# Narrower column tiles for three groups of small matmuls, with a reordered task list, in a polynomial-sketch attention and mixture-of-experts attention kernel

## The chip, the core and the metric

The kernel runs on one core of a Trainium2 chip. A core has five engines that run side by side and wait for each other through semaphores: TensorE (PE, matmuls), VectorE (DVE), ScalarE (ACT), GpSimd (POOL) and SyncE (SP, which here only issues transfers). The metric is the device time of one launch in microseconds (us). The time before is the median of three runs.

## What is computed

Two stages, for 4 batches of 1088 tokens. The first is a linear attention over 4 heads with sketched features; the second takes its output x (1088 x 128 per batch) through 4 attention experts, of which each token uses 2.

```python
# stage 1: a, b are 8-wide sketches of a token, phi their outer product (64 features)
q_p, k_p = phi(q), phi(k)
kv  = einsum('bhsf,bhsd->bhfd', k_p, v)          # sums over keys
z   = sum(k_p, axis=2)
num = einsum('bhsf,bhfd->bhsd', q_p, kv)         # numerators
den = einsum('bhsf,bhf->bhs', q_p, z) + 1e-6
x   = num / den                                  # heads side by side: (B, S, 128)
# stage 2: for each expert e of the two that a token has chosen
scores = scale * (x wq[e]) (x wk[e])^T           # causal
a      = softmax(scores)
out   += weight_of_e * (a @ (x wv[e]) @ wo[e])
```

## The kernel before

All of it is written for one core, and every engine's instructions are issued in the order of one hand-held list, ORDER. A word of the list is batch.task with arguments: `0.kv` is the task kv of batch 0. There is no scheduler behind it: an engine executes what the list gives it in that order, and waits where something it needs is late. The list mixes the batches, so that the first stage of the next batch lies between the second-stage tasks of this one.

Tasks of the first stage: `bk` and `bq` turn k and q on DVE (lines 338 to 344), `ks` and `qs` make the sketches and features (lines 370 to 411), `kv` sums over keys (kvs, line 424), `tf` turns query features on PE (line 299), `nu` makes numerators and x (numer, line 440, then DVE lines 444 to 447), `tx` turns x. `ga`, `ge` and `gw` choose two experts per token, mostly small operations on DVE and POOL; `mp` and `md` spread the choice as masks; `ld`, `sw` and `sp` issue transfers on SP: load the next batch, save x to memory, and read it back four times as xrep. `eo` and `em` multiply weights once; `warm` is a matmul whose result is not used.

Tasks of the second stage: `cu` (line 556) multiplies x by the experts' matrices and picks the two chosen ones, `s` (lines 595 and 617) makes scores, their maximum (DVE line 570) and exponentials (ACT line 574), `t` turns the weights on DVE (line 278), `vb` and `va` sum the weights times x (values, line 651), `zb` and `o` (line 733) make the output.

PE works in fp32, and each fp32 matmul is two records in the profile, each a load of weights (PEld) and a matmul. A matmul addresses a tile of the 128 x 128 array by the rows of its operands and the columns of its output. The profile writes that shape as rows*columns: `32*128` is a tile of 32 rows and 128 columns. Four tiles of 32*128 can be at work beside each other.

The task kv uses tiles of 128*64: two heads at a time, each with 64 features as weights' columns, over 33 columns of values (32 and a one for the denominator). It is 36 matmuls, 72 records, per batch. The task nu uses tiles of 64*64, 72 matmuls, 144 records, per batch.

The tasks vb and va sum over keys. Keys are split into 34 blocks of 32 tokens, c, and each block into row groups: row group r (rows 32r to 32r+31) holds 32 of every 128 queries, so that the causal end differs by r. Group B holds query tiles 1 to 5 and group A holds tiles 0, 6, 7 and 8, each tile once for each of its two chosen experts (one unit is 32 query columns). For each r and c one matmul takes xrep's block c as weights (32 rows, 128 columns) and moves 32 columns per unit that still needs block c. Towards the last blocks fewer units are left: in group A's last part the matmuls move 160, then 96, then 32 columns; in group B's last part 192, 128, then 64. The order of r is chosen greedily, by the row group that has been given the least time so far; the time counted is the larger of the columns moved and 128. The four parts of a group are the tasks vb:0 to vb:3 and va:0 to va:3, 68 records in vb:3 and 102 in va:3.

Of the kernel before, what the change touches and what calls it, by code (L numbers as in the profile page):

```python
# [19 lines left out]


ORDER = """
    0.bk 0.bq1 0.bq0 0.ks:0:4 0.vk 0.ks:4:9 0.qs:4:9 0.qs:0:4 0.tf:13:18 0.kv 0.eo 1.ld 0.tf:8:13 1.bk 0.tf:0:8
    1.ks:4:9 1.ks:0:4 0.nu:0:4 0.warm:2 0.nu:4:9 0.sw 0.tx:0:4 0.warm:2 1.bq 2.ld 0.warm:2 0.warm:2 0.ga:0:4 0.tx:4:9
    0.ge:0 0.gw:0 1.kv 0.ga:4:9 1.qs:4:9 0.em 0.mp:2:4 0.mp:4:6 1.tf:8:13 1.tf:13:18 0.mp:0:2 0.ge:4 0.sp 0.mp:6:8
    2.bk 0.mp:8:9 1.qs:0:4 2.bq 3.ld 1.nu:5:9 0.cu:4 0.cu:6 0.cu:0 0.gw:4 1.tf:0:8 2.ks:4:9 0.cu:2 0.s:5:1 1.nu:0:5
    2.ks:0:4 0.s:3 0.md 0.s:4:2 0.t:3 1.tx:0:4 0.t:5 0.t:1 2.kv 0.shb 1.tx:4:9 2.qs:4:9 2.qs:0:4 0.cu:8 0.s:7 0.s:8
    0.t:2 2.tf:13:18 0.t:4 1.ga:0:9 1.md 0.t:7 0.s:6:0 0.t:8 0.t:0 0.vb:0 0.vb:1 0.vb:2 0.vb:3 1.ge:0 2.tf:8:13 0.zb:3
    1.sw 1.cu:0 0.t:6 1.cu:4 0.o:3 1.cu:2 1.cu:6 1.s:4:2 0.zb:5 1.s:5:1 1.s:3 0.va:0 0.sha 3.bk 0.va:1 0.va:2 1.t:4
    1.t:5 2.tf:0:8 1.t:2 3.ks:0:4 3.bq 0.va:3 1.sp 1.t:1 2.nu:0:5 0.o:5 0.zb:6 1.cu:8 1.s:7 0.o:6 0.zb:0 2.tx:0:4  # L30
    1.t:3 3.ks:4:9 2.nu:5:9 1.s:6:0 0.zb:1 0.o:0 2.tx:4:9 1.s:8 1.gw:0 1.shb 0.zb:8 3.kv 2.ga:0:9 2.ge:0 1.vb:0 2.md
    2.sw 0.o:8 1.t:7 1.vb:1 3.qs:4:9 1.t:8 3.qs:0:4 1.t:0 1.t:6 1.vb:2 1.vb:3 2.cu:4 2.cu:2 0.o:1 1.zb:5 2.cu:0
    2.s:4:2 2.s:5:1 3.tf:13:18 1.sha 1.zb:3 1.va:0 1.va:1 3.tf:8:13 2.t:4 2.cu:6 1.o:3 1.o:5 2.t:1 3.tf:0:8 2.gw:0
    1.va:2 1.zb:1 2.t:5 1.va:3 3.nu:5:9 2.sp 2.s:3 2.t:2 2.s:6:0 3.nu:0:5 1.o:1 2.shb 2.t:3 3.sw 3.tx:4:9 1.zb:8
    3.tx:0:4 2.s:7 2.t:0 2.cu:8 1.o:8 3.ga:0:9 1.zb:6 1.zb:0 3.md 2.t:7 2.vb:0 2.vb:1 2.s:8 2.vb:2 2.vb:3 1.o:0 3.ge:0
    2.t:6 2.t:8 3.cu:8 3.cu:2 3.cu:4 1.o:6 2.sha 3.cu:0 3.cu:6 3.s:4:2 2.zb:5 3.s:5:1 3.t:2 3.t:1 3.s:3 2.zb:1 3.t:4
    3.t:3 2.o:5 2.zb:3 2.va:0 2.va:1 3.t:5 2.va:2 2.va:3 3.sp 3.s:8 2.o:3 2.o:1 3.gw:0 3.shb 3.t:8 2.zb:0 2.zb:6 3.s:7
    3.s:6:0 3.t:6 2.o:6 2.o:0 3.t:7 3.vb:0 3.vb:1 3.vb:2 3.t:0 3.vb:3 3.zb:1 3.va:0 3.va:1 3.va:2 3.zb:3 3.o:3 3.o:1
    3.shp 3.zb:5 2.zb:8 3.va:3 3.o:5 3.zb:0 2.o:8 3.o:0 3.zb:6 0.warm:2 3.zb:8 3.o:6 3.o:8
"""  # L40


# [1 line left out]
def kernel(  # L44
# [43 lines left out]
    P = ps.tile([128, 8, 512], F32, tag="P", name="P")  # L88
# [239 lines left out]
    def batch(b):  # L328
        if b not in made:
            made[b] = Batch(b)  # L330
        return made[b]
# [82 lines left out]
            in1=a_[:, 0, :, :, None].to_broadcast([128, n, R, R]),  # L414
            op=ALU.mult)

    def kvs(b):
        kp, k0 = batch(b).fp["k"], bank()
        kv = P[:, k0, 0 : 2 * (D + 1)].rearrange("p (m d) -> p m d", m=2)
        for m in range(2):  # L420
            for j in range(NJ):
                for x in range(2):
                    h = 2 * m + x
                    nc.tensor.matmul(kv[64 * x : 64 * x + 64, m], kp[:, j, h], vp[:, j, h, :],  # L424
                                     start=(j == 0), stop=(j == NJ - 1))
        nc.scalar.copy(kvz, kv)

    def turn_features(b, y0, y1, copy=None):
        m_ = batch(b)
# [1 line left out]
                     for y in range(y0, y1)], m_.qpT[:, y0:y1], copy)  # L431

    def numer(b, x0, x1):
        k0, m, qpT = bank(2), 2 * (x1 - x0), batch(b).qpT
        for y in range(2 * x0, 2 * x1):
            c = (D + 1) * (y - 2 * x0)
            for x in range(2):
                for half in (0, 64):
                    rows = slice(64 * x, 64 * x + 64)
                    nc.tensor.matmul(P[half : half + 64, k0 + x, c : c + D + 1], qpT[rows, y, half : half + 64],  # L440
                                     kvz[rows, y % 2], start=True, stop=True)
        den = p2.tile([128, 2, 2 * NJ], F32, tag="den", name=f"den{b}_{x0}")[:, :, 0:m]
        nus = P[:, k0 : k0 + 2, 0 : m * (D + 1)].rearrange("p x (m d) -> p x m d", d=D + 1)
        nc.vector.tensor_scalar_add(den, nus[:, :, :, D], 1e-6)
        nc.vector.reciprocal(den, den)
        for x in range(2):
            nc.vector.tensor_tensor(
                out=xs[:, x0:x1].rearrange("p j (m x d) -> p x (j m) d", m=2, x=2)[:, x], in0=nus[:, x, :, 0:D],
                in1=den[:, x, :, None].to_broadcast([128, m, D]), op=ALU.mult)
# [179 lines left out]
    def values(b, grp, part):  # L629

        tiles, units = GROUPS[grp], UNITS[grp]
        if part == 0:
            k0 = bank(2)
            held.update((k0, k0 + 1))
            k1 = bank(2)
            held.update((k1, k1 + 1))
            sums[grp] = k0, k0 + 1, k1, k1 + 1
        last = {(i, r): min(4 * i + (3 - r if i in BACK else r), NC - 1) for i in tiles for r in range(4)}
        todo = {r: collections.deque(c for c in range(*PARTS[grp][part : part + 2]) if c <= max(last[i, r] for i in tiles))
                for r in range(4)}  # L640
        time = [0] * 4
        while any(todo.values()):

            r = min((r for r in range(4) if todo[r]), key=lambda r: time[r])
            c = todo[r].popleft()
            (c0, _, u0), t = next((p, t) for p, t in zip(parts(grp), aT[grp]) if p[0] <= c < p[1])
            us = [x for x, (i, s) in enumerate(units) if c <= last[i, r]]
            assert us == list(range(us[0], len(units)))
            time[r] += max(32 * len(us), 128)
            rows = slice(32 * r, 32 * r + 32)  # L650
            nc.tensor.matmul(P[:, sums[grp][r], 32 * us[0] : 32 * len(units)], xrep[rows, c], t[rows, c - c0, us[0] - u0 :],  # L651
                             start=(c == 0), stop=(c == max(last[i, r] for i in tiles)), skip_group_check=True)
# [168 lines left out]
```

## Time and profile before

| | |
|---|---|
| median of 3 runs | 286.21 us (285.89 to 287.32) |
| the profiled execution | 287.48 us, its span 285.7 us |
| PE busy | 95% of the span, 4521 records |
| DVE / ACT / POOL busy | 77% / 37% / 21% |
| share of the chain that ended last | PE 78%, DVE 11%, transfers 4% |
| matmuls of values (line 651) | 1800 records |
| matmuls of numer (line 440) / kvs (line 424) | 576 / 288 records |

Times of the profile are microseconds from the start of the span, unless marked ns. A group of instructions is given as line, engine, operation, output<-inputs, tile, shape and type, count, then busy time, mean ns of one, and idle time before them. The chain that ended last follows the work back from the last instruction: each of its pieces has a start, the time by which it moved the end of the chain, and its engine and line. A matmul's record is longer than the time for which it keeps others out, since matmuls are pipelined; the distance between ends is what it costs.

### The profile page before, as it was taken

The page shows a single profiled execution, that of the slowest core. Times are in us where ns is not written, and L with a number is a line of the kernel's source. Part 1 is how long each engine was busy: PE and PEld are TensorE (multiplying, and loading weights), DVE is VectorE, ACT ScalarE, POOL GpSimd, SP SyncE. Part 2 cuts the span into 40 slices and gives each one's busy share as a digit, 9 for nine tenths or more (in the row PEclk, how much of TensorE's full clock was granted, in tenths as well). Part 3 has the DMA queues.
Part 4 walks back from the last instruction along what each step waited for, and adds up shares of the span by engine and source line. Part 5 has one row for each costly group of instructions (what it writes and reads, how often), then busy time and mean ns, then how long its engine had stood idle before and what let it go on. Part 6 is the DMA issues. An engine that isn't in the chain of part 4 may idle for free.

```text
span 285.7 us, 10500 instructions
## 1 busy us (share of the span) xinstructions
PE 272.0 (95%) x4521; PEld 218.3 (76%) x4521; DVE 220.4 (77%) x499; ACT 105.2 (37%) x262; POOL 59.3 (21%) x143
## 2 busy tenths in 40 slices
PE   7789699999999999999999999999999999999993
PEld 2776588756599769877797699678796797589983
DVE  5916859888788988988594968885988997986541
ACT  2242373384533282055212542353133622250110
POOL 8516052323311002221460021003001001000100
PEclk9979959999999999999999999999999999999999
DMA  6930999803415002692157032994433108923011
GB/s 211 266 71 22 286 184 193 187 7 126 96 31 177 21 0 71 125 181 48 33 94 196 8 49 50 164 165 97 105 122 66 22 11 156 181 52 91 12 39 38
DMA packets 41086, 28.94 MB, mean 101 GB/s; under 512 B 7504, under 2 KB 39504, under 8 KB 41040
## 3 DMA queue, kind: packets, MB, share of 16 engines
q1 hardware_dynamic: 41024, 28.28, 45.9%
q8 instruction: 35, 0.57, 0.9%
q14 instruction: 11, 0.09, 0.1%
q10 hardware_dynamic: 16, 0.00, 0.0%
HBM read 23.66 MB, written 4.60 MB: 99 GB/s over the span
## 4 chain that ended last, share of the span: by engine, by line
PE 78%; DVE 11%; DMA 4%; issue 2%; POOL 2%; ACT 0%; SPq 0%; POOLq 0%; DVEq 0%; ACTq 0%
PE P L651 23%; PE P L595 22%; PE P L733 10%; PE P L556 9%; PE P L440 3%; PE P L299 3%; PE P L401 2%; PE P L617 2%; DMA mk<-dm 2%; PE P L424 2%; DVE qT L344 2%; DMA dm<-sel 1%; DVE zT L726 1%; DVE a L570 1%; POOL qp L411 1%
## 5 line engine op out<-in xcount | busy, mean ns | idle before, releaser
L574 ACT ACTIVATE a<-a,mx 128x768 f32<-128x768 f32 (+8 forms) x68 | 53.8, 791 | 67.0 <-DVE mx L570 56.7
L595 PE MATMUL P<-xT,uT 128*128 128x512 f32 (+3 forms) x192 | 64.9, 490 | 0.2
L595 PEld LDWEIGHTS P<-xT,uT 128*128 128x128 f32 x192 | 34.0, 190 | 26.4 <-issue 18.4
L651 PE MATMUL P<-aTA,xrep 32*128 32x160 f32 (+3 forms) x1080 | 39.1, 295 | 0.0
L651 PEld LDWEIGHTS P<-aTA,xrep 32*128 32x128 f32 x1080 | 37.9, 185 | 1.3 <-DVE mx L570 0.8
L733 PEld LDWEIGHTS P<-mo,zT 128*128 128x128 f32 (+1 forms) x288 | 33.9, 185 | 4.6 <-issue 1.9
L733 PE MATMUL P<-mo,zT 128*128 128x128 f32 (+1 forms) x288 | 36.6, 279 | 0.8 <-DVE zT L726 0.7
L651 PE MATMUL P<-aTB,xrep 32*128 32x320 f32 (+4 forms) x720 | 37.2, 348 | 0.0
L570 DVE CUSTOM_DVE_ANT_0 a<-P,mask 128x768 f32<-128x768 f32 (+3 forms) x32 | 32.4, 1018 | 4.4 <-PE P L595 4.0
L651 PEld LDWEIGHTS P<-aTB,xrep 32*128 32x128 f32 x720 | 33.1, 185 | 3.3 <-issue 1.0
L556 PE MATMUL P<-xT,mcat 128*128 128x256 f32 (+1 forms) x160 | 33.6, 361 | 0.0
L556 PEld LDWEIGHTS P<-xT,mcat 128*128 128x128 f32 x160 | 27.5, 190 | 3.7 <-issue 0.5
L278 DVE STREAM_TRANSPOSE aTA<-a 128x256 f32<-128x256 f32 (+4 forms) x28 | 24.4, 916 | 1.6 <-ACT a L574 1.6
L278 DVE STREAM_TRANSPOSE aTB<-a 128x1024 f32<-128x1024 f32 (+3 forms) x28 | 24.4, 910 | 0.5 <-ACT a L574 0.5
L562 DVE COPY_PREDICATED uT<-mk,P 128x512 f32<-128x512 uint8 (+1 forms) x30 | 18.5, 637 | 7.7 <-DMA mk<-dm 4.6
L736 ACT COPY ob<-P 128x256 f32<-128x256 f32 (+2 forms) x24 | 7.5, 313 | 39.6 <-PE P L733 36.3
L726 DVE COPY_PREDICATED zT<-mk,yT 128x768 f32<-128x768 uint8 (+2 forms) x24 | 18.6, 775 | 3.9 <-POOL zT L723 1.7
L724 DVE TENSOR_TENSOR zT<-yT,mk 128x768 f32<-128x768 f32 (+2 forms) x24 | 17.0, 710 | 3.0 <-PE P L733 2.9
L411 POOL TENSOR_TENSOR kp<-kab 128x1280 f32<-128x1280 f32 (+1 forms) x6 | 13.0, 2173 | 21.1 <-DVE kab L408 12.9
L558 ACT COPY uT<-P 128x512 f32<-128x512 f32 (+1 forms) x20 | 10.3, 522 | 16.3 <-PE P L556 16.2
L570 DVE CUSTOM_DVE_ANT_0 a<-P,mask_back 128x256 f32<-128x256 f32 (+3 forms) x32 | 15.2, 484 | 0.0
L411 POOL TENSOR_TENSOR qp<-qab 128x1280 f32<-128x1280 f32 (+1 forms) x6 | 12.9, 2173 | 8.5 <-DVE qab L408 5.9
(190 smaller groups left out, 298.8 us busy)
## 6 DMA issues: line engine op xcount, KB each, us to landing
xrep<-dx SPq DMA_DIRECT2D x16, 544.0 KB, 9.0
mk<-dm SPq DMA_DIRECT2D x4, 864.0 KB, 6.0
kin<-in_k_dram SPq DMA_DIRECT2D x4, 544.0 KB, 4.1
qin<-in_q_dram SPq DMA_DIRECT2D x4, 544.0 KB, 8.0
vin<-in_v_dram SPq DMA_DIRECT2D x16, 128.0 KB, 6.8
dx<-xs SPq DMA_DIRECT2D x4, 512.0 KB, 6.6
out_dram<-ob SPq DMA_DIRECT2D x64, 16.0 KB, 2.1
out_dram<-ob SPq DMA_DIRECT2D x16, 64.0 KB, 1.6
```

The lines of the kernel that those rows point to most:

```text
L278: nc.vector.transpose(t[:, 0 : c1 - c0, n - u0 : n - u0 + s].rearrange("p c s k -> p s c k"), a[:, :, 32 * c0 : 32 * c1].rearrange("p s (c ...
L411: eng.tensor_tensor(out=fp[:, j0:j1].rearrange("p j h (x y) -> p (j h) x y", y=R), in0=a_[:, 1, :, None, :].to_broadcast([128, n, R, R]), ...
L556: nc.tensor.matmul(P[:, k0 + x // 2, x % 2 * w : x % 2 * w + w], mcat[:, e], queries, start=True, stop=True)
L558: nc.scalar.copy(u.rearrange("p t s q -> p s t q"), P[:, k0, 0 : 2 * w].rearrange("p (s t q) -> p s t q", s=2, t=n))
L562: nc.vector.copy_predicated(u, mk[:, :, :, x].bitcast(U8), c[:, :, None].to_broadcast([128, n, 2, q]))
L570: nc.vector.tensor_tensor_reduce(out=dst, in0=src, in1=msk, scale=-1.0, scalar=most, op0=ALU.add, op1=ALU.min, accum_out=mx)
L574: nc.scalar.activation(out=a, in_=a, func=ACTF.Exp, bias=mx, scale=-1.0, accum_out=z)
L595: nc.tensor.matmul(flat[:, f + c : f + c + n], turned(b, i)[:, s], m_.xT[:, c - at[i] : c - at[i] + n], start=True, stop=True)
L651: nc.tensor.matmul(P[:, sums[grp][r], 32 * us[0] : 32 * len(units)], xrep[rows, c], t[rows, c - c0, us[0] - u0 :], start=(c == 0), stop=(c ...
L724: nc.vector.tensor_tensor(out=z[:, :, 0:X], in0=y[:, :, 0, None].to_broadcast([128, n, X, nq]), in1=mk[:, :, 0:X], op=ALU.mult)
L726: nc.vector.copy_predicated(z[:, :, 1:], mk[:, :, X:].bitcast(U8), y[:, :, 1, None].to_broadcast([128, n, X, nq]))
L733: nc.tensor.matmul(P[0:nq, k0, DM * t : DM * t + DM], self.zT[:, t, e], mo[:, e], start=(e == 0), stop=(e == E - 1))
```

## The change

Three tasks use narrower tiles, and the list is new.

kvs and numer take 32 columns of weights at a time for batches 1 to 3 (batch 0 keeps 64): kv is 72 matmuls of 128*32 instead of 36 of 128*64, and nu 144 of 64*32 instead of 72 of 64*64 per batch. The task kv may be given in two halves (`1.kv:0:1`, `1.kv:1:2`), each with its own copy to kvz.

In values, where one unit is left, the 128 columns of xrep are taken as four matmuls of 32*32; where two or three are left, as two of 32*64; else as before. The time counted in choosing the row group is now the columns moved, without the floor of 128. Its matmuls per batch go from 34 to 50 in vb:3 and from 51 to 106 in va:3; the other parts are unchanged.

The list has the same tasks in another order, with three `warm` words instead of five and kv of the later batches in halves. Batch 0's `vk` and `kv` are earlier, `eo`, the second half of its gate (`0.ga:0:4`) and part of its masks later, after the first `cu`; the loads of batches 2 and 3 are issued on SP ahead of batch 0's `sw` and `sp`. Behind batch 3's last `va:3` stand 3.zb:0, 2.o:6, 3.o:0, 3.zb:6, 3.o:6, 3.zb:8 and 3.o:8, where there were also 3.o:5, 2.o:8 and a `warm`.

```diff
 ORDER = """
-    0.bk 0.bq1 0.bq0 0.ks:0:4 0.vk 0.ks:4:9 0.qs:4:9 0.qs:0:4 0.tf:13:18 0.kv 0.eo 1.ld 0.tf:8:13 1.bk 0.tf:0:8
-    1.ks:4:9 1.ks:0:4 0.nu:0:4 0.warm:2 0.nu:4:9 0.sw 0.tx:0:4 0.warm:2 1.bq 2.ld 0.warm:2 0.warm:2 0.ga:0:4 0.tx:4:9
-    0.ge:0 0.gw:0 1.kv 0.ga:4:9 1.qs:4:9 0.em 0.mp:2:4 0.mp:4:6 1.tf:8:13 1.tf:13:18 0.mp:0:2 0.ge:4 0.sp 0.mp:6:8
-    2.bk 0.mp:8:9 1.qs:0:4 2.bq 3.ld 1.nu:5:9 0.cu:4 0.cu:6 0.cu:0 0.gw:4 1.tf:0:8 2.ks:4:9 0.cu:2 0.s:5:1 1.nu:0:5
+    0.bk 0.vk 0.bq0 0.warm:2 0.warm:2 0.bq1 0.ks:0:4 0.ks:4:9 0.qs:4:9 0.qs:0:4 0.kv 1.ld 0.tf:8:13 0.tf:13:18
+    0.tf:0:8 0.nu:4:9 0.em 1.bk 1.ks:0:4 1.ks:4:9 1.bq 0.tx:4:9 2.ld 0.nu:0:4 0.ga:4:9 0.ge:4 1.kv:0:1 0.tx:0:4
+    0.mp:4:6 0.mp:6:8 0.gw:4 1.kv:1:2 2.bk 1.qs:0:4 1.qs:4:9 2.bq 3.ld 0.cu:6 0.cu:4 0.ga:0:4 0.eo 1.tf:13:18 1.tf:0:8
+    0.mp:8:9 0.sw 0.mp:0:2 0.sp 1.tf:8:13 0.ge:0 0.mp:2:4 0.gw:0 0.cu:2 2.ks:0:4 0.cu:0 2.ks:4:9 1.nu:5:9 1.nu:0:5
...
-    def kvs(b):
-        kp, k0 = batch(b).fp["k"], bank()
+    def kvs(b, m0=0, m1=2):
+
+        kp, k0, w = batch(b).fp["k"], bank(), 32 if b else 64
...
-        for m in range(2):
+        for m in range(m0, m1):
             for j in range(NJ):
-                for x in range(2):
-                    h = 2 * m + x
-                    nc.tensor.matmul(kv[64 * x : 64 * x + 64, m], kp[:, j, h], vp[:, j, h, :],
+                for x in range(0, 128, w):
+                    h = 2 * m + x // 64
+                    nc.tensor.matmul(kv[x : x + w, m], kp[:, j, h, x % 64 : x % 64 + w], vp[:, j, h, :],
                                      start=(j == 0), stop=(j == NJ - 1))
-        nc.scalar.copy(kvz, kv)
+        nc.scalar.copy(kvz[:, m0:m1], kv[:, m0:m1])
...
-            for x in range(2):
-                for half in (0, 64):
+            for q in range(0, 128, w):
+                for x in range(2):
                     rows = slice(64 * x, 64 * x + 64)
-                    nc.tensor.matmul(P[half : half + 64, k0 + x, c : c + D + 1], qpT[rows, y, half : half + 64],
+                    nc.tensor.matmul(P[q : q + w, k0 + x, c : c + D + 1], qpT[rows, y, q : q + w],
                                      kvz[rows, y % 2], start=True, stop=True)
...
-            time[r] += max(32 * len(us), 128)
-            rows = slice(32 * r, 32 * r + 32)
-            nc.tensor.matmul(P[:, sums[grp][r], 32 * us[0] : 32 * len(units)], xrep[rows, c], t[rows, c - c0, us[0] - u0 :],
-                             start=(c == 0), stop=(c == max(last[i, r] for i in tiles)), skip_group_check=True)
+            time[r] += 32 * len(us)
+            rows, w = slice(32 * r, 32 * r + 32), {1: 32, 2: 64, 3: 64}.get(len(us), 128)
+            for d in range(0, DM, w):
+                nc.tensor.matmul(P[d : d + w, sums[grp][r], 32 * us[0] : 32 * len(units)], xrep[rows, c, d : d + w],
+                                 t[rows, c - c0, us[0] - u0 :], start=(c == 0), stop=(c == max(last[i, r] for i in tiles)),
+                                 skip_group_check=True)
```

## The prediction

> **What bounds the kernel now.** I read the page's busy shares and slices first, then busy times by stretch, then the chain that ended last, then groups by shape, then single records where one tile shape follows another.
>
> ```profile
> PE 272.0 (95%) x4521; PEld 218.3 (76%) x4521; DVE 220.4 (77%) x499; ACT 105.2 (37%) x262; POOL 59.3 (21%) x143
> PE   7789699999999999999999999999999999999993
> PEclk9979959999999999999999999999999999999999
> ```
>
> TensorE has holes only in the first six slices and at the end. The stretches show it (columns: stretch, its length, busy time of PE, PEld, DVE, ACT, POOL, clock, transfers):
>
> ```profile
> 43.40:78.20 34.80, 34.80 (x512) 23.85 (x512) 30.59 (x77) 18.55 (x46) 11.82 (x11) 1.00 0.56 122
> 180.00:230.00 50.00, 50.00 (x609) 38.43 (x605) 41.72 (x95) 21.25 (x53) 4.78 (x20) 1.00 0.51 104
> 230.00:278.00 48.00, 47.96 (x799) 41.34 (x795) 35.34 (x63) 10.15 (x27) 3.50 (x18) 1.00 0.43 81
> ```
>
> From 43.4 to 278 us PE never stops, at full clock, and no other engine does. So a PE microsecond added there is a microsecond of the span, and its savings count too as long as DVE (42 of 50 us at most) keeps up.
>
> Now what a matmul costs. The chain's pieces (start, time by which the end moved, what):
>
> ```profile
> 56.80 0.49 PE P L401 x32
> 112.17 0.62 PE P L401 x32
> 117.46 1.09 PE P L733 x8
> 226.02 0.89 PE P L733 x8
> 63.05 2.22 PE P L424 x72
> 73.96 0.71 PE P L476 x63
> 125.80 0.91 PE P L440 x64
> 226.91 9.34 PE P L651 x249
> ```
>
> The reader should compare equal work after different neighbours. The 32 records of L401 (64*64) take 0.49 us behind numer (also 64*64), 0.62 behind L299 (64*128). The 8 records of L733 (128*128) take 0.89 behind scores of the same shape, 1.09 behind numer. A change of shape costs 0.13 us into 64 columns and 0.20 into 128, also where only the columns differ (64*128 to 64*64). The records show why:
>
> ```profile
> 73.54 0.41 PE L299 MATMUL P<-ident,qp 64*128 64x64 f32 x8
> 73.89 0.21 PE L476 MATMUL P<-wg,xT 128*32 128x4 f32 x3
> 73.61 0.20 PEld L299 LDWEIGHTS P<-ident,qp 64*128 64x128 f32 x4
> 73.88 0.12 PEld L476 LDWEIGHTS P<-wg,xT 128*32 128x32 f32 x3
> ```
>
> The new shape's first weights load at 73.88, after all matmuls of the old one have started and 0.07 us before the last ends. In every change of shape after 43 us, also between the 128-column and 64-column outputs of L733, it is this 0.07 us. Within one shape, loads run ahead of matmuls. The first 32-column result comes at about 74.08, 0.12 us after the old shape's end (73.96).
>
> ```profile
> L651 PE MATMUL P<-aTA,xrep 32*128 32x96 f32 x128 | 7.3, 266 | 0.0
> L651 PE MATMUL P<-aTA,xrep 32*128 32x32 f32 x104 | 5.4, 263 | 0.0
> ```
>
> Matmuls of 32 columns take as long as those of 96 (263 and 266 ns): the 128 weight columns set the pace. That waste is what the change is about.
>
> **Part 1, the narrow ends of values.** First the pace. Batch 2's group A (four parts, 9.34 us less one entry of 0.2) moves in its busiest row group 1184+1120+1120+1888 = 5312 columns, each matmul counted as at least 128: 1.7 ns a column. In va:3 it has by the loop 7 matmuls of 160, 4 of 96 and 2 of 32 columns: 7x160 + 4x128 + 2x128 = 1888, times 1.7 = 3.2 us, and va:3 indeed lasts 3.0 to 3.4. Without the floor it is 7x160 + 4x96 + 2x32 = 1568, or 2.7. For vb:3 1280 becomes 1024: 2.2 to 1.7. Were that all, the four batches would save 4 x (0.55 + 0.45) = 3.9 us.
>
> But the greedy choice interleaves row groups that are at different widths. I worked va:3's loop through: 16 matmuls of 128 columns, then single ones or pairs whose widths run 64, 128, 64, 128, 64, 128, 64, 32, 64, 32, 64, 32, 64, 32, 64, 32, 64, 32, 64, 32, 64, 32. These are 22 changes of shape per part: 3 into 128, 11 into 64, 8 into 32. vb:3 has 5: 2 into 128, 3 into 64.
>
> If each change waits as in the records above, va:3 becomes a row of short stretches. Entries: 3x0.20 + 11x0.14 + 8x0.12 = 3.1 us (0.14 between 0.13 and the 0.16 that numer's 64 records pay elsewhere). Work inside, that of the busiest row group: 128 columns 4x0.267 + 3x0.267 = 1.87; 64 columns at 96 moved, two records of 0.08 each, 10 stretches with one matmul and one with two, 1.92; 32 columns, at 33 ns a record (L476: (0.71-0.12) over 72 records on four tiles) and 7 ns from one tile to the next, four stretches of one, three of two, one of three matmuls: 4x0.087 + 3x0.153 + 0.22 = 1.03. With 0.1 for the second halves: 8.0 us, against 3.2. Plus 4.8 per batch, 19.2 in all.
>
> vb:3: entries 2x0.20 + 3x0.14 = 0.82; 128 columns 0.96 + 2x0.21; 64 columns at 61 ns a record (0.49 us over 8 rounds of four), busiest row groups 1, 2 and 4 matmuls, 14 records, 0.85: 3.05, against 2.1. Plus 0.95 per batch, 3.8 in all. Part 1: **+23.0 us**. Nothing hides it, PE being full. Ends: -3.9 (a change among column widths costs nothing), and with the entries a quarter dearer, 4 x 3.9 x 0.25 = 3.9 more, +27.
>
> [...] The trace has no 32-row tile beside one of another width; for 64 and 128 rows it shows the drain.
>
> **Part 2, kvs.** Now 72 records at 2.22 us with entry. New: 144 records of 128*32, four tiles; the nearest row is L476 (128*32, 4 columns moved instead of 33): 0.59/72 = 8.2 ns a record, so 1.18 + 0.12 = 1.3. Saves 0.9, three times, 2.7; the halves are apart for batches 1 and 3, two entries more: **-2.4**. Ends: at 61/4 ns as for 64 columns 144 records take 2.2 and save nothing; at L476's pace without entries -3.
>
> **Part 3, numer.** Now 64 records in 0.91 and 80 in 1.30 us, 144 records. New: 288 records on eight tiles; a start follows another by about 7 ns at best in this trace (8.2 for L476), so 2.0 to 2.4 plus two entries, against 2.2: **0**, ends -0.5 and +1.5 for the three batches. The matmul stream is then limited by starts, so halving the width saves nothing.
> [...]
>
> **Part 4, the list.** Changes of shape between tasks go from 82 to 84: +0.3. At the start, the page's groups show PE idle for 8.7 us, before L543 (2.1, behind the gate's selb on DVE), L370 (1.7), L160 (1.1), L299 (0.9 and 0.6), L424, L466 and L440. The first two starts stay. The new list lets `cu` begin after one half of the gate, but puts eo, 0.ga:0:4, two tf's, masks and 1.nu:5:9 behind it, about 8 us of PE work, and on DVE kT (1.45) and qT (2.25) of batch 1 now stand between numer and the gate. Following the DVE order by hand, I get the first `cu` near 33 us instead of 43.4 and a PE wait near 41 us for 0.mp:8:9, whose selb stands behind qT and two copies of `cu`. I take **-1.5**. Ends: -7 (all idle but the first two starts, 5.9, and about 1 for the sixth slice, which ran at half clock), +4 (kT and qT uncovered). On SP, the loads of batches 2 and 3 now stand ahead of 0.sw; these wait for DVE's qT of batch 2 (about 38 us), so xrep lands around 50 instead of 43, while the first vb starts about 78: no cost. ACT gets two copies of 0.2 us, at 37% busy no cost; POOL, 21% busy, the same work. At the end DVE's yT, zb:0 and zb:6 stand between va:3 and 3.o:6 as before; 2.o:6 and 3.o:0 (2.9 us) replace 3.o:5, 2.o:8, 3.o:0 (3.0) as cover: 0.
>
> **Sum.** 287.48 (profiled run) + 23.0 - 2.4 + 0 + 0.3 - 1.5 = 306.9; this run lies 1.27 above the median of 286.21, so **305.6 us** against the median.
>
> **The rivals.** First, *tile widths mix freely in 32-row tiles* (or each row group empties only for itself: then 2 changes in the longest row group, +0.26 and +0.14, give back 1.6). 286.2 - 3.9 - 2.4 + 0.3 - 1.5 = 278.7, or 280.3. For it: four row groups' loads start 7 ns apart and run beside each other. Against: the changes between 64*128 and 64*64, same rows, wait. It decides below 7.5/108 = 0.07 us for each of the 108 changes within the parts. Chance 0.11.
> Second, *the list removes nearly all the head's waits* while part 1 costs what I say: 305.6 - 5.5 = 300. Chance 0.14. Third, *the list adds waits*, because it was laid out for shorter parts, or qT stands uncovered: 305.6 + 5.5 = 311. Against: longer PE parts give DVE more time. Chance 0.13. A fourth, that half of each wait is covered by other row groups: 305.6 - (23.0 + 3.9)/2 = 292, 0.06; nothing in the trace shows a half wait. The forecast itself: 0.56.
>
> **How the numbers follow.** Slower by over 0.5% (about 1.4 us, what can be told from no change) are the forecast and the second to fourth, 0.89, less 0.01 for a fourth that goes further: 0.88. Faster is the first rival less 0.01: 0.10; same 0.02. The low end leaves out the first and the fourth rival, 0.17, and takes in the second with the entries a little cheaper: 296; the high end takes the dearer entries (+4) and the third: 315. If the forecast's mechanism holds alone, 300 to 311.
>
> **What would show it.** va:3 near 8 us and vb:3 near 3 in each batch, in 32*64 and 32*32 groups with PEld idle before them; kvs 1.3 us; numer still about 2.2; no new DVE waits after 50 us. Wrong if records of 32*64 overlap those of 32*128: then va:3 is under 3 us and the time falls.

## The result, and the profile after

The changed kernel takes **338.87 us** (median of 4 runs, 337.14 to 343.75) against 286.52 us (median of 4) for the kernel before on the same chip: 1.1805 times the time before, interval 1.1746 to 1.1864. The forecast was 305.6 us, in a range of 296 to 315. The direction was right; the loss is 52.4 us, not 19. A median here is of all runs; a ratio and its interval leave out runs in a slower state, at a lower clock (343.75 us at 0.903 of full speed, the others at 0.907 to 0.924).

Line numbers of values, numer and kvs in the changed kernel are 653, 441 and 425. First the page of the changed kernel: busy times, the slices of PE and of its granted clock, and the queue that brings instructions (packets, MB, share).

```profile
PE 311.7 (93%) x5733; PEld 240.2 (71%) x5733; DVE 220.8 (66%) x499; ACT 106.8 (32%) x265; POOL 58.8 (17%) x143
...
PE   7977891699999999799999999999999999999994
...
PEclk9976995599999995979999995999999859999969
...
q8 instruction: 45, 0.74, 1.0%
```

Three things differ from the page before. PE is busy for 39.7 us more and has a hole in the seventh and eighth slices (1 and 6 tenths). The granted clock, which was at full speed from the seventh slice on, falls to 5 to 9 tenths again and again up to the end; by the trace's records of the clock some 48 us between 43 us and the last PE record run at half speed. And 45 instruction packets came instead of 35: 16.4 KB each (0.74 MB over 45). The page of the kernel before has:

```profile
q8 instruction: 35, 0.57, 0.9%
```

The stretches (columns: stretch, its length, busy time of PE, PEld, DVE, ACT, POOL, clock, transfers, GB/s) are of 0.va:3, 1.va:3, the scores behind it, and 1.nu:

```profile
121.50:131.10 9.60, 9.60 (x217) 6.72 (x213) 3.92 (x5) 1.52 (x3) 0.00 (x0) 0.80 0.35 69
195.20:204.10 8.90, 8.90 (x217) 6.29 (x213) 2.86 (x9) 1.48 (x3) 1.21 (x5) 0.90 0.26 57
204.10:210.20 6.10, 6.10 (x17) 3.27 (x14) 1.94 (x5) 1.07 (x3) 0.00 (x0) 0.59 1.17 181
48.90:62.60 13.70, 3.18 (x294) 2.92 (x288) 2.53 (x8) 0.49 (x2) 3.90 (x3) 0.62 0.92 141
```

The same stretches of the kernel before, 1.va:3 and scores:

```profile
175.70:179.00 3.30, 3.30 (x113) 3.26 (x107) 2.70 (x4) 0.00 (x0) 0.00 (x0) 1.00 0.17 45
180.10:185.40 5.30, 5.30 (x20) 2.74 (x20) 4.65 (x13) 1.97 (x5) 0.00 (x0) 1.00 1.12 193
```

1.va:3 has gone from 3.3 to 8.9 us. PE counts as busy for all of it, but PEld only for 6.29 of 8.90, where it was 3.26 of 3.30. Behind it the scores run at 0.59 of the clock beside the same kind of transfer (1.17 and 1.12) that left the clock at 1.00 before. And 1.nu takes 13.7 us with PE busy for 3.18.

PEld's idle time in 1.va:3 stands mostly before the narrow groups. The last number of a line is idle time before the group, with what ended it; the first line is of all values tasks of group A in the kernel before, the others of 195.2 to 202.2 in the changed one:

```profile
L651 PEld LDWEIGHTS P<-aTA,xrep 32*128 32x128 f32 x1080 | 37.9, 185 | 1.3 <-DVE mx L570 0.8 <-issue 0.2
L653 PEld LDWEIGHTS P<-aTA,xrep 32*128 32x128 f32 x44 | 2.0, 184 | 0.4
L653 PEld LDWEIGHTS P<-aTA,xrep 32*64 32x64 f32 x56 | 1.9, 130 | 0.9 <-issue 0.7
L653 PEld LDWEIGHTS P<-aTA,xrep 32*32 32x32 f32 x64 | 1.0, 104 | 0.7
```

Cut at the clock's own steps, the end of 1.va:3 and what follows looks so:

```profile
198.90:202.30 3.40, 3.40 (x96) 2.28 (x96) 0.65 (x1) 0.00 (x0) 0.00 (x0) 1.00 0.12 35
202.30:205.70 3.40, 3.40 (x50) 2.03 (x51) 1.25 (x2) 0.00 (x0) 0.00 (x0) 0.50 1.10 195
205.70:209.10 3.40, 3.40 (x7) 1.77 (x6) 1.10 (x3) 0.00 (x0) 0.00 (x0) 0.50 1.18 186
209.10:212.50 3.40, 3.40 (x173) 2.87 (x171) 2.19 (x8) 2.47 (x5) 0.27 (x2) 1.00 1.18 176
```

The clock falls to exactly half at 202.3, after 7 us of short stretches, and stays there for two steps of 3.4 us, most of them in work that the change did not touch. The busy column shows nothing of it.

Single records of PE in the first numer after batch 0 (start, busy time, group, idle time before it):

```profile
48.90 1.27 PE L441 MATMUL P<-kvz,qpT 64*32 64x33 f32 x127
56.32 1.55 PE L441 MATMUL P<-kvz,qpT 64*32 64x33 f32 x128 [6.15 <-issue]
62.25 0.50 PE L441 MATMUL P<-kvz,qpT 64*32 64x33 f32 x33 [4.37 <-issue]
```

The two waits end for no semaphore ("issue"), and between them lie 128 records, which are 256 instructions (a load of weights and a matmul each). A packet of the instruction queue, 16.4 KB, would be just these by the counts: 45 packets came for 11466 records of PE and PEld (2x5733), 255 to each, and 35 for 9042 in the kernel before, 258 to each (an estimate, since the profile does not name the engine that a packet serves). 256 instructions, the 128 records of PE between two such waits, are called a block below, and such waits are called waits for instructions. Two such packets ran at 53.3 to 54.7 and 59.5 to 60.9; PE went on about 1.5 us after each.

Where the time went, task by task (the distance between the ends of the tasks' last PE records, summed over the batches):

| tasks | after less before, us | forecast |
|---|---|---|
| va:3 | +23.8 | +19.2 |
| vb:3 | +5.0 | +3.8 |
| nu, batches 1 to 3 | +15.0, of which 12.9 waits for instructions | 0 |
| s, o, cu (the same work as before) | +7.1, +3.9, +1.5 | 0 |
| kv, batches 1 to 3 | -0.2 | -2.4 |
| the rest, mostly before 45 us | -5.2 | -1.2 |

The sum, before rounding, is +51.0: the last PE record ends 51.0 us later, and the span is 51.1 us longer.

The clock accounts for the row of s, o and cu. These tasks spend 25.2 us at half clock, where they spent none before; half of that, 12.6 us, is what they lost (12.5). Of the 25.2 us, 18.4 lie behind the va:3 tasks, 6.4 behind numer's waits (in 52.1 to 65.8 and 144.3 to 147.7), and 0.4 at the start.

### The profile page after: what moved, and what is told of

Same layout as the page of the kernel before. It is cut to its first block, busy times and chain, and to the rows that moved or that the text cites. A ratio compares the mean times of both kernels' runs of the same rounds, so it can differ in the third digit from the quotient of the medians.

```text
span 336.8 us, 12916 instructions
## 1 busy us (share of the span) xinstructions
PE 311.7 (93%) x5733; PEld 240.2 (71%) x5733; DVE 220.8 (66%) x499; ACT 106.8 (32%) x265; POOL 58.8 (17%) x143
## 4 chain that ended last, share of the span: by engine, by line
PE 87%; DVE 5%; issue 5%; DMA 1%; SPq 1%; ACT 0%; ACTq 0%; DVEq 0%
PE P L653 31%; PE P L596 21%; PE P L736 10%; PE P L557 9%; PE P L441 3%; PE P L401 3%; PE P L618 2%; PE P L299 2%; PE P L425 2%; PE P L370 1%; DVE qT L344 1%; PE P L544 1%; DVE uT L563 1%; SPq L744 1%; PE P L477 1%
## 5 line engine op out<-in xcount | busy, mean ns | idle before, releaser
L575 ACT ACTIVATE a<-a,mx 128x896 f32<-128x896 f32 (+8 forms) x68 | 54.0, 795 | 96.9 <-DVE mx L571 96.7
L596 PE MATMUL P<-xT,uT 128*128 128x512 f32 (+3 forms) x192 | 72.7, 533 | 0.0
L653 PE MATMUL P<-aTA,xrep 32*128 32x160 f32 (+3 forms) x1520 | 62.5, 281 | 0.0
L653 PEld LDWEIGHTS P<-aTA,xrep 32*128 32x128 f32 (+2 forms) x1520 | 50.6, 161 | 12.7 <-issue 7.1
L653 PE MATMUL P<-aTB,xrep 32*64 32x64 f32 (+4 forms) x848 | 41.6, 325 | 0.0
L571 DVE CUSTOM_DVE_ANT_0 a<-P,mask 128x640 f32<-128x640 f32 (+3 forms) x32 | 32.6, 1019 | 12.4 <-PE P L596 11.9
L653 PEld LDWEIGHTS P<-aTB,xrep 32*128 32x128 f32 (+1 forms) x848 | 35.5, 169 | 6.3 <-issue 1.8
L441 PE MATMUL P<-kvz,qpT 64*32 64x33 f32 (+1 forms) x1008 | 12.4, 215 | 12.9 <-issue 12.9
L441 PEld LDWEIGHTS P<-kvz,qpT 64*32 64x32 f32 (+1 forms) x1008 | 11.2, 119 | 15.1 <-issue 13.3
L727 DVE TENSOR_TENSOR zT<-yT,mk 128x768 f32<-128x768 f32 (+2 forms) x24 | 17.1, 713 | 5.5 <-PE P L736 5.3
L571 DVE CUSTOM_DVE_ANT_0 a<-P,mask_back 128x384 f32<-128x384 f32 (+3 forms) x32 | 15.4, 485 | 4.1 <-PE P L596 4.1
## 6 DMA issues: line engine op xcount, KB each, us to landing
vin<-in_v_dram SPq DMA_DIRECT2D x16, 128.0 KB, 4.9
```

Source lines behind the costliest of these rows:

```text
L441: nc.tensor.matmul(P[q : q + w, k0 + x, c : c + D + 1], qpT[rows, y, q : q + w], kvz[rows, y % 2], start=True, stop=True)
L571: nc.vector.tensor_tensor_reduce(out=dst, in0=src, in1=msk, scale=-1.0, scalar=most, op0=ALU.add, op1=ALU.min, accum_out=mx)
L575: nc.scalar.activation(out=a, in_=a, func=ACTF.Exp, bias=mx, scale=-1.0, accum_out=z)
L596: nc.tensor.matmul(flat[:, f + c : f + c + n], turned(b, i)[:, s], m_.xT[:, c - at[i] : c - at[i] + n], start=True, stop=True)
L653: nc.tensor.matmul(P[d : d + w, sums[grp][r], 32 * us[0] : 32 * len(units)], xrep[rows, c, d : d + w], t[rows, c - c0, us[0] - u0 :], star ...
L727: nc.vector.tensor_tensor(out=z[:, :, 0:X], in0=y[:, :, 0, None].to_broadcast([128, n, X, nq]), in1=mk[:, :, 0:X], op=ALU.mult)
```

## The experiments

All kernels compute the same function and leave nothing out. Each time stands against the kernel before on the same chip (286.2 to 286.7 us). The expectations name theories by letters. A: the drains between widths (waits at a change of shape, where the new shape's first load starts only 0.07 us before the old one's last end) make the loss, with the slower clock behind them, and the list is nearly free. B: the list makes much of it. C: the number of PE instructions as such does. D: instructions come late because a large transfer, xrep, runs beside numer. E: they come late without it as well. F: the half clock comes from long runs of drains, so that dense work between them keeps the clock up. G: it does not.

### One part at a time

**The list alone**, with all old widths:

```diff
-        k0, m, qpT, w = bank(2), 2 * (x1 - x0), batch(b).qpT, 32 if b else 64
+        k0, m, qpT, w = bank(2), 2 * (x1 - x0), batch(b).qpT, 64
...
-            time[r] += 32 * len(us)
-            rows, w = slice(32 * r, 32 * r + 32), {1: 32, 2: 64, 3: 64}.get(len(us), 128)
+            time[r] += max(32 * len(us), 128)
+            rows, w = slice(32 * r, 32 * r + 32), 128
```

(part of the diff against the changed kernel; in kvs the width is 64 too)

> The new list with the tile widths of before in kvs, numer and values (the halves of kv stay). Theory A (shape changes inside values, the half clock that follows them, and numer's wait for instructions make the loss; the list alone does little): 283 to 288 us, ratio 0.99 to 1.005, no PE wait over 1 us behind 45 us. Theory B (the list holds a large part of the loss, by laying the transfer of xrep beside numer and by what it uncovers): over 295 us, with a wait at 1.nu even at 64 columns.

295.31 us, 1.0208 [1.0121, 1.0296], so 6 us by the ratio and 8.6 by the medians: above what A gave, at the edge of B's bound, and worse than the -1.5 us forecast for the list. Its PE records at 1.nu:

```profile
51.01 1.20 PE L441 MATMUL P<-kvz,qpT 64*64 64x33 f32 x71
54.04 2.24 PE L441 MATMUL P<-kvz,qpT 64*64 64x33 f32 x73 [1.83 <-issue]
```

Even with 64 columns, 1.nu in the new list waits 1.83 us for instructions, and 2.nu 0.74; in the start 17.1 us run at half clock (19.6 to 36.7, behind a wait of 2.46 us for instructions at 17.5), where it was 3.4 and 6.8, and 6.8 more fall on the first scores. So the list has a cost of its own.

**Values alone**, old list:

```diff
-            time[r] += max(32 * len(us), 128)
+            time[r] += 32 * len(us)
+            rows, w = slice(32 * r, 32 * r + 32), {1: 32, 2: 64, 3: 64}.get(len(us), 128)
+            for d in range(0, DM, w):
...
```

> The list, kvs and numer of before; only values takes its narrow ends by 32 and 64 columns. Theory A: va:3 about 8 us at full clock and up to 9.5 where the clock halves in it, vb:3 3.2 to 3.4, so +23 to 29 us directly, and stretches of half clock behind each va:3 for another 6 to 10: 316 to 326 us. Theory C (the loss in values is one of the number of instructions, 10500 to about 11600, not of shapes): va:3 stretched evenly, with PE waiting for issue, 295 to 305.

324.91 us, 1.1316 [1.1227, 1.1405], as theory A had it: the narrow ends are the largest part. Its trace, by stretches: two steps of the clock inside 1.va:3 (183.9 to 193.0), and the second half of 3.va:3 with the output behind it:

```profile
186.90:190.30 3.40, 3.40 (x100) 2.32 (x90) 0.00 (x0) 0.00 (x0) 0.00 (x0) 1.00 0.00 0
190.30:193.70 3.40, 3.40 (x99) 2.54 (x92) 1.25 (x2) 0.00 (x0) 0.00 (x0) 0.50 1.04 198
...
303.00:313.20 10.20, 10.20 (x143) 7.63 (x139) 2.77 (x5) 0.53 (x2) 0.52 (x2) 0.50 0.03 10
```

The clock halves inside the run of drains here too. In the last line it stays at 0.50 for 10.2 us with hardly a transfer (0.03), so a low clock does not need one. va:3 takes 9.97, 8.90, 9.58 and 10.24 us, +25.8 in all, vb:3 +4.4; scores, output, numer and cu, whose work is the same, +9.6.

**The changed kernel with values as before**, the counterpart:

```diff
-            time[r] += 32 * len(us)
-            rows, w = slice(32 * r, 32 * r + 32), {1: 32, 2: 64, 3: 64}.get(len(us), 128)
+            time[r] += max(32 * len(us), 128)
+            rows, w = slice(32 * r, 32 * r + 32), 128
```

> The changed kernel with values as before (kvs and numer stay at 32 columns, the list is new). Theory A: gives back 23.8 us of va:3, 5 of vb:3 and some 8 of half clock behind them: 299 to 305 us, with numer's waits at batch 1 and 2 (6.2, 4.4 and 2.4 us) still there. Theory C: gives back less than half of the loss, over 315.

312.95 us, 1.0899 [1.0824, 1.0975]. That is above A's 305 and a little under C's bound. Numer is why: its waits for instructions are 6.36 and 4.37 us at 1.nu, 3.92 at 2.nu and 3.74 at 3.nu, 18.4 in all, more than the 12.9 in the changed kernel itself. So without the narrow values some 26 us of loss remain, and values, which alone cost 38.2, give only 26 back here; 5.5 of the difference are numer's waits.

**kvs alone**, old list, 32 columns for batches 1 to 3:

```diff
-        kp, k0 = batch(b).fp["k"], bank()
+        kp, k0, w = batch(b).fp["k"], bank(), 32 if b else 64
...
```

> The kernel before with kvs alone at 32 columns for batches 1 to 3 (whole, not in halves). By the changed kernel's pieces (0.74 and 0.64 us for two halves) 1.3 to 1.4 instead of 2.2 us three times: 283.5 to 285 us, ratio 0.99 to 0.995. If its denser instructions (288 in 1.3 us) wait for their blocks: 286 to 291.

288.64 us, 1.0053 [1.0012, 1.0094]: in the worse of the two expected bands. The task shrank: 2.kv takes 1.36 us where it was 2.22, 1.kv 1.82 with a wait of 0.24 for instructions in it, and 3.kv 1.94 (before 2.07) with a wait of 0.35. But behind 1.kv, PE stops:

```profile
28.55 0.32 PE L401 MATMUL P<-SKW,qT 64*64 64x64 f32 x3
33.54 1.33 PE L401 MATMUL P<-SKW,qT 64*64 64x64 f32 x37 [4.67 <-issue]
```

4.67 us for instructions, while the loads of later batches run. 0.83 more are lost at 66 us. The total rose by only 1.5 us by the ratio (2.4 by the medians), about 0.5%; the profiled run's span is even 0.2 us shorter. Part of the wait takes the place of another: the mp tasks behind it, which waited for selb, take 3.2 us less than before.

**kvs for batches 2 and 3 only**, to keep the saving clear of the start:

```diff
-        kp, k0, w = batch(b).fp["k"], bank(), 32 if b else 64
+        kp, k0, w = batch(b).fp["k"], bank(), 32 if b > 1 else 64
```

(diff against the run before)

> The kernel before with kvs at 32 columns for batches 2 and 3 alone; batch 1, whose kv lies among the loads at the start, stays at 64. The run with all three gained 1.8 us in kvs and lost it again in a wait of 0.8 us behind 2.kv and one of 4.7 behind 1.kv. If only the latter eats the gain: 284.5 to 285.5 us, ratio 0.993 to 0.998. If blocks come late behind 2.kv and 3.kv too: 286 to 288.

293.44 us, 1.0261 [1.0213, 1.0309]: slower than either expectation, and slower than with batch 1 narrow as well. 2.kv:

```profile
60.41 1.42 PE L425 MATMUL P<-vp,kp 128*32 128x33 f32 x142
63.44 0.25 PE L425 MATMUL P<-vp,kp 128*32 128x33 f32 x2 [1.61 <-issue]
```

A wait of 1.61 us for two last records, with no transfer running. There are two more waits for instructions, 1.74 at 2.nu beside a transfer (share 1.18) and 2.55 at 138 us without one (0.01), each followed by half clock (at 128.0 and 141.7, 3.4 us each). The three waits are 5.9 of the 6.9 us lost; a half clock of 6.8 us can make up to 3.4 more. Why the ends of blocks fall worse here than with batch 1 narrow stays open.

**numer alone**, old list:

```diff
-        k0, m, qpT = bank(2), 2 * (x1 - x0), batch(b).qpT
+        k0, m, qpT, w = bank(2), 2 * (x1 - x0), batch(b).qpT, 32 if b else 64
...
```

> The kernel before with numer alone at 32 columns for batches 1 to 3, in the old list. There xrep of batch 1 is issued just ahead of 2.nu:0:5, while 1.nu and 3.nu:5:9 have no such transfer ahead. Theory D: a wait of 2 to 5 us at 2.nu:0:5 and half clock behind it, none at 1.nu, perhaps one at 3.nu:0:5: 289 to 297 us. Theory E: all three batches slower by the same, 4 us or more each, over 298. Forecast's part 3 (no cost): 286 to 288.

303.45 us, 1.0577 [1.0501, 1.0652]: outside what D gave, within E's band, though not with the same loss in every batch, as E had it. 2.nu:0:5:

```profile
116.84 0.35 PE L441 MATMUL P<-kvz,qpT 64*32 64x33 f32 x31
118.05 1.28 PE L441 MATMUL P<-kvz,qpT 64*32 64x33 f32 x128 [0.86 <-issue]
126.72 0.26 PE L441 MATMUL P<-kvz,qpT 64*32 64x33 f32 x1 [7.38 <-issue]
```

160 records take 10 us, 8.2 of it waiting; the one record behind the last block's end waits 7.38. xrep of batch 1 was issued at 116.6 to 119.1, the next instruction packet ran at 123.9 to 125.2. 1.nu:5:9, 128 records at 41.3 to 42.8, had no wait, although a transfer ran beside it (share 1.19 from 40 to 44): where the end of a block falls decides too. So the number of instructions may make the wait, and the transfer beside it may make it long; the next runs take that apart.

### The pace of instructions

**Each numer matmul twice** at 64 columns, in the old list with old values and kvs: as many instructions as narrow numer, but no new tile shape. The diff is against the changed kernel's numer, with its width set to 64.

```diff
+                    for _ in range(2 if b else 1):
-                    nc.tensor.matmul(P[q : q + w, k0 + x, c : c + D + 1], qpT[rows, y, q : q + w],
-                                     kvz[rows, y % 2], start=True, stop=True)
+                        nc.tensor.matmul(P[q : q + w, k0 + x, c : c + D + 1], qpT[rows, y, q : q + w],
+                                         kvz[rows, y % 2], start=True, stop=True)
```

> The kernel before, with numer at 64 columns but every matmul of numer issued twice for batches 1 to 3 (the second writes the same sums again): as many PE instructions as with 32 columns, in tiles of the old shape. Theory D (instruction blocks late beside the xrep transfer): 2.nu:0:5 ends as late as with 32 columns, 8 to 10.5 us, with waits after 128 records each, and 3.nu:0:5 near 4: 297 to 306 us. Theory E (64*32 tiles are slow by themselves): 2.2 us more per batch and no wait over 1 us: 291 to 294.

304.74 us, 1.0635 [1.0566, 1.0703], as expected.

```profile
115.93 0.69 PE L442 MATMUL P<-kvz,qpT 64*64 64x33 f32 x31
117.17 2.11 PE L442 MATMUL P<-kvz,qpT 64*64 64x33 f32 x128 [0.55 <-issue]
125.01 0.31 PE L442 MATMUL P<-kvz,qpT 64*64 64x33 f32 x1 [5.74 <-issue]
```

The same pieces of 31, 128 and 1 records, and waits in the same places (0.55 and 5.74 us for 0.86 and 7.38). They do not need the 32-column tile.

**The changed kernel with xrep of batch 0 later**, out of 1.nu's way:

```diff
-    0.mp:8:9 0.sw 0.mp:0:2 0.sp 1.tf:8:13 0.ge:0 0.mp:2:4 0.gw:0 0.cu:2 2.ks:0:4 0.cu:0 2.ks:4:9 1.nu:5:9 1.nu:0:5
-    1.sw 0.s:4:2 0.md 0.s:3
+    0.mp:8:9 0.sw 0.mp:0:2 1.tf:8:13 0.ge:0 0.mp:2:4 0.gw:0 0.cu:2 2.ks:0:4 0.cu:0 2.ks:4:9 1.nu:5:9 1.nu:0:5
+    1.sw 0.s:4:2 0.sp 0.md 0.s:3
...
```

> The changed kernel with one word moved: batch 0's read-back of x into xrep (0.sp) is issued behind 1.nu and the first score task instead of ahead of them. Theory D (numer's waits are late instruction blocks, which queue behind the four xrep transfers of 544 KB): the waits of 6.2 and 4.4 us at 1.nu go, with them a part of the 13.7 us of half clock there: 322 to 330 us; the next dense task beside the transfer (2.kv) may wait instead. Theory E (64*32 tiles are slow by themselves, or wait for ACT's copies): 1.nu stays over 10 us, 336 to 341.

333.38 us, 1.1661 [1.1583, 1.1739]: between the two bands. Records of 1.nu, and the stretch around it:

```profile
48.64 1.27 PE L441 MATMUL P<-kvz,qpT 64*32 64x33 f32 x127
51.70 1.28 PE L441 MATMUL P<-kvz,qpT 64*32 64x33 f32 x128 [1.79 <-issue]
55.43 0.50 PE L441 MATMUL P<-kvz,qpT 64*32 64x33 f32 x33 [2.44 <-issue]
```

```profile
49.00:57.00 8.00, 3.77 (x260) 2.93 (x257) 3.11 (x11) 0.23 (x2) 3.54 (x3) 0.82 0.03 6
```

With nothing but instruction packets on the queues (share 0.03) the waits are 1.79 and 2.44 instead of 6.15 and 4.37. So both theories hold a part: about 2 us a block without a transfer in this task, and 3.4 and 1.8 times that beside one. 6.3 us were won at 1.nu and 5.5 in the total.

**The changed kernel with numer at 64 columns**:

```diff
-        k0, m, qpT, w = bank(2), 2 * (x1 - x0), batch(b).qpT, 32 if b else 64
+        k0, m, qpT, w = bank(2), 2 * (x1 - x0), batch(b).qpT, 64
```

> The changed kernel with numer at 64 columns in all batches. Theory D: half as many instructions in numer, so the block is needed later; waits like those of the list-only run (1.8 and 0.7 us) instead of 6.2, 4.4 and 2.4, and less half clock: 318 to 326 us. Theory E: numer falls to 2.2 us per batch without any wait, 316 to 322.

330.93 us, 1.1575 [1.1493, 1.1657], above the expected band. 1.nu still waits 5.32 us, once instead of twice, since xrep is beside it in this list; and 0.va:3 took 11.57 us. So undoing numer in the changed kernel gives back 8 us, not the 12.9 of its waits.

**numer alone, xrep of batches 1 and 2 issued later**, first behind the numer tasks, then behind the output tasks that follow them (2.sp likewise, behind 3.nu:0:5 and then behind 1.o:1; the diffs show part of one line of the list):

```diff
-    0.va:3 1.sp 1.t:1 2.nu:0:5 0.o:5 0.zb:6
+    0.va:3 1.t:1 2.nu:0:5 1.sp 0.o:5 0.zb:6
```

> Numer alone at 32 columns in the old list, as in the earlier run, with two words moved: the read-backs of x for batches 1 and 2 (1.sp, 2.sp) are issued behind 2.nu:0:5 and 3.nu:0:5 instead of ahead. Theory D: the waits of 7.4 and 2.3 us shrink to under 1.5 each, and the half clock behind them goes: 289 to 295 us. Theory E: as the earlier run, 300 to 306.

299.93 us, 1.0467 [1.0377, 1.0556]: the edit did not move the transfer. SP runs ahead of PE and waits only for the data of what it issues; xrep was issued at 115.2, before 2.nu was through, and the wait of 6.84 us remained.

```diff
-    0.va:3 1.sp 1.t:1 2.nu:0:5 0.o:5 0.zb:6
+    0.va:3 1.t:1 2.nu:0:5 0.o:5 1.sp 0.zb:6
```

> Numer alone at 32 columns in the old list, with the read-backs of batches 1 and 2 placed on SP behind the output transfers of 0.o:5 and 1.o:1, which exist only after 2.nu:0:5 and 3.nu:0:5 (in the run before, the moved words left the transfers where they were, since SP waits for data, not for PE's place in the list: xrep was issued at 115.2 us as ever). Theory D: without a transfer beside it, a block still comes late, but by 1.8 to 2.4 us as where 0.sp was moved in the changed kernel: 2.nu:0:5 3 to 5 us instead of 9.5 to 10, 3.nu:0:5 at most 4, less half clock: 290 to 297 us. If the transfer has no part in it: 2.nu:0:5 stays over 8 us and the time at 299 to 306.

307.85 us, 1.0775 [1.0667, 1.0884]. The task itself did what D said:

```profile
115.32 1.54 PE L441 MATMUL P<-kvz,qpT 64*32 64x33 f32 x159
118.87 0.21 PE L441 MATMUL P<-kvz,qpT 64*32 64x33 f32 x1 [2.01 <-issue]
...
204.34 1.40 PE L653 MATMUL P<-aTB,xrep 32*128 32x320 f32 x2 [4.14 <-DMA xrep<-dx]
207.30 1.43 PE L653 MATMUL P<-aTB,xrep 32*128 32x320 f32 x2 [1.55 <-DMA xrep<-dx]
```

One wait of 2.01 us where there were 8.2. The total missed, since batch 2's xrep, behind the output transfers on SP, was now issued only from 198.7 on: 2.vb:0 waits 8.9 us for it in four pieces, and 17.1 us at half clock follow from 202.1. The run settles the wait, not a better place for the transfer.

### The drains and the clock

**Values alone, sorted by width**: each part does its 128-column matmuls first, then 64, then 32. The same instructions, two changes of width instead of 22.

```diff
+        wide = lambda r: {1: 32, 2: 64, 3: 64}.get(sum(todo[r][0] <= last[i, r] for i, s in units), 128)
...
-            r = min((r for r in range(4) if todo[r]), key=lambda r: time[r])
+            r = min((r for r in range(4) if todo[r]), key=lambda r: (-wide(r), time[r]))
```

> As the run with narrow values alone, the same matmuls, but each part does all its 128-column matmuls first, then those of 64, then those of 32: 2 changes of shape in va:3 instead of 22, 1 in vb:3 instead of 5. Theory A: va:3 3.1 us, vb:3 1.9, no half clock behind them, 284 to 287 us. Theory C (number of instructions): as the run with narrow values alone, over 295.

300.40 us, 1.0476 [1.0413, 1.054]: 24.5 us less than unsorted, but far above what A gave, and past C's bound. Batch 1's va:3 by shape:

```profile
L654 PE MATMUL P<-aTA,xrep 32*64 32x96 f32 x64 | 1.5, 249 | 0.0
L654 PE MATMUL P<-aTA,xrep 32*32 32x32 f32 x104 | 1.1, 195 | 0.0
```

This task takes 4.4 us, against 8.2 unsorted at full clock: 0.19 us for each of 20 changes that are gone. (The 8.2 is an estimate, since the clock halves within va:3 in every unsorted run: 7.0 us of 1.va:3 in the changed kernel, up to 202.3, and 1.2 for its last four stretches by the time of equal ones before.) But it was 3.2 with wide tiles. By the ends of their records the 64 of 32*64 take 1.41 us, 22 ns each, and the 104 of 32*32 take 1.07, 10.3 ns each. They replace 16 and 13 wide matmuls, 4 and 3.25 in each row group; at the prediction's 1.7 ns for each of 128 columns these are 0.87 and 0.71 us. The two times hold one change each, 0.14 and 0.12 at the prediction's prices. So the narrow tiles are dearer even without the drains. The task now uses up blocks of instructions quickly as well: waits of 0.52, 2.00 (at 2.nu, which follows) and 1.24 us. Half clock between 43 us and the last PE record fell from 41.0 to 13.7 us, and part of that lies beside and behind these waits. That more instructions cost by themselves (theory C) is so in part; that sorting makes the narrow ends pay is refuted.

**Values alone, cut in two**: dense tasks of about 1.9 us between the two halves of the old va:3. In the other batches these are 2.s:3, 3.s:8, and 3.o:5 with 2.o:8. (The diff, against values alone, shows part of one line of the list.)

```diff
-    PARTS = {"B": (0, 4, 8, 14, 24), "A": (0, 7, 14, 21, 34)}
+    PARTS = {"B": (0, 4, 8, 14, 24), "A": (0, 7, 14, 21, 28, 34)}
...
-    0.va:3 1.sp 1.t:1 2.nu:0:5 0.o:5 0.zb:6 1.cu:8
+    0.va:3 0.o:5 1.cu:8 0.va:4 1.sp 1.t:1 2.nu:0:5 0.zb:6
```

> Narrow values alone in the old list, with group A's last part cut in two at block 28 and a dense task (outputs or scores of 1.9 us) between the halves. The greedy order begins anew at the cut, so 13 changes of shape per batch instead of 22. By the changes alone (0.19 us each, from sorted against mixed: 3.7 us for 20): 9 x 4 x 0.19 = 7 us less than 324.9, so 318. Theory F (half clock follows a run of drains of several us, as va:3's 8 us): the halves of 2.5 to 4 us no longer trip it, and up to 16 us more come back: 302 to 311. Theory G (half clock follows the number of drains or instructions, however cut): 315 to 322.

306.01 us, 1.0679 [1.0607, 1.0752], as F had it, 18.9 us less than uncut. Batch 1's va:3, the dense task, and va:4:

```profile
179.90:183.50 3.60, 3.60 (x73) 2.56 (x67) 2.60 (x3) 0.00 (x0) 0.00 (x0) 1.00 0.08 23
183.50:185.30 1.80, 1.80 (x4) 0.60 (x4) 0.70 (x2) 0.00 (x0) 0.00 (x0) 1.00 0.00 0
185.30:187.90 2.60, 2.60 (x152) 1.93 (x152) 1.27 (x3) 1.63 (x4) 0.00 (x0) 1.00 0.07 20
```

```profile
PEclk9999699999999999799999999999999999999999
```

The clock stays at 1.00 through all three stretches, and between 43 us and the last PE record only 3.4 us run at half clock instead of 41.0. The greedy order starts afresh in va:4, which leaves 13 changes instead of 22: va:3 and va:4 take 6.1 us instead of the estimated 8.2 at full clock, some 8 us over four batches. The other 11 are the clock's by this estimate. The run has both fewer changes and dense work between them, so it does not show how much of the clock either keeps alone.

Alone, the four parts cost by the medians 38.2 (values), 17.2 (numer), 2.4 (kvs) and 6 to 9 us (list), some 65 together; combined they cost 52.4. How the 52.4 divides among them beyond the table above stays open, since the waits move with every edit. No version was found that beats the kernel before.

## Why the prediction was right and wrong

**Right: Part 1's mechanism and its price at full clock.** Changes among column widths of 32-row tiles do drain. In 1.va:3 of the changed kernel, before 202.3, a 64-column stretch with one matmul in its busiest row group takes 0.31 to 0.32 us from end to end (forecast 0.14 + 2x0.08 = 0.30) and one with two 0.48 (forecast 0.14 + 4x0.08 = 0.46); a 32-column stretch with one 0.19 (0.21), with two 0.26 (0.27); a 128-column one with one 0.46 to 0.48 (0.47). The new shape's first load starts 0.07 us before the old one's last end in these changes as well. The four batches at full clock give (8.2 - 3.2)x4 = 20.0 by the estimate above and with vb:3's 5.0 about 25.0, forecast 23.0. The first rival (widths mix freely, 278.7 us) and the half wait (292) fall.

**Wrong: "From 43.4 to 278 us PE never stops, at full clock ... So a PE microsecond added there is a microsecond of the span".** This step took the full clock for granted while it put 8 us of drains into the stretch. In each such run the clock halves, within the task and in what follows: 9.2 us in s, o and cu (half of the 18.4 at half clock behind va:3), and 23.8 - 20.0 = 3.8 in va:3. It also halves beside and behind numer's waits, for another 3.2 us in s and o. Of the 31.6 us by which the table's 51.0 exceed the forecast in it (19.4), the clock is 16.2 and numer's waits are 12.9. Values cut in two, with dense work between and fewer changes, kept the clock, so a shorter run with fewer changes does not have this price. Half-clock stretches are 3.4 us or multiples of it in every run (3.41, 6.83, 10.24 and 13.65 us in the changed kernel), but for the last one, which the trace's end cuts. Why the clock halves beside drains and waits, and what sets these lengths, no run here shows.

**Wrong: Part 3's "0" for numer, bounded at -0.5 and +1.5.** It was +15.0. The work without its waits is 2.1 us more than before over three batches, a little above the upper bound, some of it at half clock; 128 records take 1.27 us at full clock, 10 ns a record, where the forecast had 7 to 8.2. What failed is that only PE's own pace was bounded, not its supply. The row that Part 3 leaned on, L476, has 72 records, 144 instructions, less than a block of 256, and could not show it. In the kernel before, the longest waits for instructions are 0.78 and 0.70 us; where PE used up a block in 1.3 to 2.1 us, a wait was 1.6 to 2.4 us without a transfer and up to 7.4 beside one.

**Wrong: Part 4's -1.5 and "xrep lands around 50 instead of 43 ... no cost".** The first `cu` started at 34.54 (forecast near 33), and PE waited for 0.mp:8:9's selb where I said (0.76 us at 41.3). But xrep's transfer now ran beside 1.nu, and I asked only who waits for xrep, not who shares the queues with it. The list alone costs 6 to 9 us, of which 2.6 are waits in numer; half clock at the start and in the first scores is part of the rest, not separated further. The second and third rivals spoke of waits on DVE; the waits that came were for instructions.

**Part 2's -2.4 was right for the task and wrong for the kernel.** In batches 2 and 3 the pieces of kvs take 0.64 to 0.76 us, 1.4 and 1.5 per batch (forecast 1.3). But 1.kv takes 3.4 us, with a wait of 1.05 us for POOL's kp and its second half at half clock, so that the three batches together save 0.2. Kvs alone brought no gain (+1.5 us by the ratio), since waits for instructions came with it.

**What would show it**: va:3 near 8 (8.8 to 9.5, by the estimate 8.2 at full clock), vb:3 near 3 (3.2 to 3.4) and PEld idle before the narrow groups all came; numer at 2.2 did not.

## What to carry to other kernels

Price a small-tile edit three times: by the drains between shapes (0.19 us for each change here), by the instructions that it adds per microsecond (a block of 128 fp32 matmul records that PE used up within 1.3 us was followed by a wait here), and by the clock, since 18.4 us of the work behind the four va:3 (8.8 to 9.5 us each, drains included) ran at half clock here, though PE read as 100% busy. Where a rearranged list moves a large transfer, look at who runs beside it as well as at who waits for it. Halving the columns of small matmuls saved 0.9 us a batch in kvs and nothing in numer, and doubled their instructions.

## What the runs showed that I had not expected

- PE's instructions came in packets of 16.4 KB, about 256 instructions each by the counts (an estimate: 45 packets for 11466 records). Where numer went through one in 1.3 to 2.1 us, PE waited 1.8 to 2.4 us for the next with idle queues and 3.7 to 7.4 us beside xrep's transfer, at 32 and at 64 columns. Where fewer than 100 records lay between the task's start and the end of a block, the wait was 0.5 to 3.9 us, and some numer tasks of 128 or 160 records had none.
- The clock fell to half in 6.8 to 13.7 us long stretches inside and behind 9 to 10 us of drains, with PE busy for 100% of the time and with as little as 0.03 of transfer share. 1.9 us of dense work in the middle of the run, with 13 changes left of 22, removed nearly all of it.
- Sorted and without drains, tiles of 32*64 with 96 columns moved still cost 22 ns a record, and 32*32 10.3 ns: 1.41 and 1.07 us in 1.va:3, where the wide matmuls that they replace come to 0.87 and 0.71 at 1.7 ns a column (an estimate).
